# Attention with one ring of seven PSUM banks and an exponential for each score

## The chip, the core and the metric

The kernel runs on one core of a Trainium2 chip. A core has five engines that run their own instruction streams and meet through semaphores: TensorE (PE in the profile, its weight loads PEld), VectorE (DVE), ScalarE (ACT), GpSimd (POOL) and SyncE (SP), which here issues most of the transfers. Matrix products land in PSUM, here used as eight banks of 128 x 512 fp32; VectorE and ScalarE read them from there. The metric is the time of one execution on the device in microseconds; less is better.

## What is computed

A transformer block on x of shape 1 x 2048 x 448: attention with 16 query heads of 28 that share one key and one value head, and beside it an MLP, both on a layer norm of x, summed with x.

```python
x = A_x
xn = _layernorm(x, axis=-1)
return x + _A_ref(xn, A_wq, A_wk, A_wv, A_wo) + _B_ref(xn, B_w1, B_b1, B_w2, B_b2)
# _A_ref
q = (lambda x, *d: x.transpose(*d))((x @ wq).reshape(B, S, H, Dh), 0, 2, 1, 3)
k = x @ wk
v = x @ wv
scores = jnp.einsum("bhqd,bkd->bhqk", q, k) * (Dh ** -0.5)
p = _softmax(scores, axis=-1)
o = jnp.einsum("bhqk,bkd->bhqd", p, v)
return (lambda x, *d: x.transpose(*d))(o, 0, 2, 1, 3).reshape(B, S, H * Dh) @ wo
# _B_ref
y = _layernorm(x, axis=-1)
h = _gelu(jnp.einsum("bsd,df->bsf", y, w1) + b1)
return jnp.einsum("bsf,fd->bsd", h, w2) + b2
```

## The kernel before

Everything is fp32; most products use a rounded high part and a remainder. The order of each engine's work is written out by hand: instructions go to the engines' queues in the order of the Python program.

**Stages.** First layer norms and the projections to queries, keys and values (queries are parked in DRAM, `qd`). Then the MLP, with part of the attention's preparation woven in. Last, from about 500 us on, the attention stage, which alone is changed. It works in 16 units, each 512 query rows by a group of four heads, and each unit walks the 2048 keys in blocks of 128 (`kt`), two blocks per step: 128 steps, eight per unit.

**What a step issues.**
- *Scores* (`scores`, `one_score`, `single`; tile `s` or `m`): one matmul of a block of 128 keys with 512 queries of one head, then an exponential on ScalarE into half of a tile `p` (128 x 2 x 512; 13 of these, `PAIRS`). `scores` puts two scores into one tile `s` of two banks and takes one exponential over 1024 columns (L869). `single` takes one bank `m` and one exponential over 512 columns (L847); its two halves of a `p` are filled by two successive calls, kept in `halfway`. In the last `LEAD` = 11 steps the last pair of an odd step is taken apart in this way too (L862).
- *Maxima* (`max_stream`, L507 to L513; tile `m`): softmax needs each row's maximum ahead. A matmul gives 512 scores of 128 queries, and VectorE reduces them (L509). Sixteen per head; they run many units ahead of use, and the last eleven steps have none. Letter `m`.
- *Turned scores* (`turned_scores`, L541 to L549): for the fourth head of the units in `TURNED` (1 to 15) the scores are made with the queries on the partitions; VectorE writes them to SBUF with their maximum, ScalarE takes the exponential there (`turned_exp`, L560), and they go through DRAM (`td`) back as `half`. Letter `t` is one such matmul, `x` one exponential with, every second time, four stores issued from SP. The steps behind the last tile have no `t`.
- *Turned blocks* (`turn_blocks`, L834): VectorE transposes two blocks of `half` into a `p` tile. Letter `T`, two calls in an even step. So a unit in `TURNED` has six scores per step (three heads, two blocks) and takes the fourth head from `T`; unit 0 has eight scores.
- *PV* (`pv`, L820; letter `P`, only in even steps): four blocks of 128 keys with all four heads, 16 fp32 products that the profile lists as 32 matmuls, into the bank `po`. Each even step's burst takes the four blocks of the two steps before it.
- *Side work*: `n` is one move of the normalisation of a finished unit (`norm_jobs`: a copy of `po` by ScalarE, small transfers on the POOL queue, products on GpSimd), `o` one of the output projection (`o_jobs`: 12 matmuls into one bank `m`, an addition on VectorE, L735, and a store), `e` prepares the next unit's maxima (`load_max`: one transpose into a bank `m`, a copy on ScalarE and one on VectorE).

**PSUM.** In the attention stage: three banks `m` (pool `mp`, opened at the start of the kernel and shared by maxima, turned scores, singles, output projection and transposes), two tiles `s` of two banks each (pool `sp`), one bank `po` (pool `op`). A tile of a pool is given out in rotation; the matmul that writes it waits for the reader of the tile that had the bank before.

**Order.** `ORDERS[u in TURNED][n % 2]` (L29) holds one letter per piece of work: first the orders for unit 0, then for the others, each for even and odd steps; `p` is a pair of scores and `s` a single one. Maxima are dealt out by `weight` (L882): an `m` is skipped when enough of them are done for the share of the steps passed.

Of the kernel before, what the change touches and what calls it, by code (L numbers as in the profile page):

```python
# [8 lines left out]
F32 = mybir.dt.float32  # L9
F32R = mybir.dt.float32r  # L10
AF = mybir.ActivationFunctionType
ALU = mybir.AluOpType
AX = mybir.AxisListType
PSUM = bass.MemoryType.PSUM
# [11 lines left out]
BURST = 4  # L26
PAIRS = 13
MLP_MAX = 18
ORDERS = (("nmpmpmtpnompmTxP", "nmpmmpmpmepmon"), ("nsmptponmmsTxP", "nmpmmpmepmon"))  # L29
TURNED = tuple(range(1, 16))  # L30
RAWS = 2
GELU = 0.044715, 0.7978845608028654
# [6 lines left out]
def block_kernel(ctx, tc, x, wq, wk, wv, wo, w1, b1, w2, b2, out):  # L39
# [5 lines left out]
        return t.bitcast(F32)  # L45

    keep = ctx.enter_context(tc.tile_pool(name="keep", bufs=1))
    mp = ctx.enter_context(tc.tile_pool(name="mp", bufs=3, space=PSUM))
    dram = ctx.enter_context(tc.tile_pool(name="dram", bufs=1, space=bass.MemoryType.DRAM))
    xt_p = ctx.enter_context(tc.tile_pool(name="xt", bufs=2))  # L50
    qmp = ctx.enter_context(tc.tile_pool(name="qmp", bufs=1))
# [1 line left out]
    def heads_of(u):  # L53
        return 3 if u in TURNED else 4
# [56 lines left out]
    def mtile(shape):  # L111
        return mp.tile(shape, F32, name="m")
# [576 lines left out]
                    maxed += mxs.step()  # L689
    ph1b.close()  # L690
    ph1.close()

    att = ctx.enter_context(tc.tile_pool(name="att", bufs=2))
    sp = ctx.enter_context(tc.tile_pool(name="sp", bufs=2, space=PSUM))
    op = ctx.enter_context(tc.tile_pool(name="op", bufs=1, space=PSUM))

    wor = att.tile([P, NG, D], F32, name="wor", bufs=1)
# [134 lines left out]
    def turn_blocks(u, kt):  # L832
        p = pair_of()
        dve.transpose(p.rearrange("p k (g j) -> p g k j", j=32),  # L834
                      halves[u, kt // 8][:, :, 32 * (kt % 8):32 * (kt % 8) + 64].rearrange("p g (k j) -> p g k j", j=32))
        ps[u, kt, 3], ps[u, kt + 1, 3] = p[:, 0], p[:, 1]

    def pair_of():
        return att.tile([P, 2, CW], F32, name="p", bufs=PAIRS)

    halfway = []

    def one_score(u, kt, job, p):
        k, j = job
        s = mtile([P, CW])
        pe.matmul(s, ks[:, (kt + k) * P:(kt + k + 1) * P], qss[u][:, j, :], start=True, stop=True)  # L846
        act.activation(p, s, AF.Exp, scale=SCALE)  # L847
        ps[u, kt + k, j] = p

    def single(u, kt, jobs):  # L850
        if not halfway:
            halfway.extend((jobs.pop(), pair_of()))
            one_score(u, kt, halfway[0][0], halfway[1][:, 0])
        else:
            pair, p = halfway
            halfway.clear()
            one_score(u, kt, pair[1], p[:, 1])

    def scores(u, kt, jobs, apart):
        p = pair_of()  # L860
        if apart:
            for i in range(2):  # L862
                one_score(u, kt, jobs[i], p[:, i])
            return
        s = sp.tile([P, 2, CW], F32, name="s")
        for i, (k, j) in enumerate(jobs):
            pe.matmul(s[:, i], ks[:, (kt + k) * P:(kt + k + 1) * P], qss[u][:, j, :], start=True, stop=True)  # L867
            ps[u, kt + k, j] = p[:, i]
        act.activation(p, s, AF.Exp, scale=SCALE)  # L869

    def o_wait(c, gs, tiles):
        for k in range(4):
# [6 lines left out]
    pvq = [(u, kt) for u in range(NU) for kt in range(NT)]  # L879
    total = 4 * CT * len(heads)  # L880
    left = total - maxed
    weight = [0 if n >= len(steps) - LEAD else (3, 5)[n % 2] + (u == 0) for n, (u, kt) in enumerate(steps)]  # L882
    for n, (u, kt) in enumerate(steps):
        if n == 0:
            loads = pool
        if n == len(steps) - 14:
            load_rows_of(NCH - 1, range(CT))
        if u + 1 < NU and kt in ((8, 14) if u else (0, 4)):
            load_d(u + 1, kt in (4, 14))
        if 4 <= n < 4 + NG:  # L890
            prep_wo(n - 4)
        if u + 1 < NU and kt < 8:
            load_q(u + 1, (kt // 2,))
        jobs = [((0, 0), (0, 1)), ((0, 2), (1, 2)), ((1, 0), (1, 1))]
        if u not in TURNED:
            jobs[1:2] = [((0, 2), (0, 3)), ((1, 2), (1, 3))]
        for what in ORDERS[u in TURNED][n % 2]:
            if what == "s":
                single(u, kt, jobs)
            elif what == "p":  # L900
                scores(u, kt, jobs.pop(0), n % 2 == 1 and n >= len(steps) - LEAD and len(jobs) == 0)
            elif what == "m":
                if maxed < total - left + left * sum(weight[:n + 1]) / sum(weight):
                    maxed += mxs.step()
            elif what == "t":
                tq.step()
            elif what == "x":
                turned_exp()
            elif what == "T":
                for k in range(2 if u in TURNED else 0):  # L910
                    turn_blocks(u, kt + 2 * k)
            elif what == "e":
                if kt == (6 if u + 2 < NU else 10) and u + 1 < NU:
                    load_max(u + 1)
            elif what == "n":
                side.step()
            elif what == "o":
                if n == len(steps) - 5:
                    oside.add(o_jobs(NCH - 1, range(NG - 1)))
                oside.step()  # L920
            elif what == "P":
                for _ in range(BURST if n else 0):
                    pv(*pvq.pop(0))
    while pvq:
# [28 lines left out]
```

## Time and profile before

Three timed executions took 1139.23, 1139.19 and 1136.71 us, median 1139.19. The profiled execution took 1138.7 us, of which 1136.9 us lie between the first and the last instruction (its span). Busy time of each engine in stretches of the span:

| stretch (us) | what runs | PE | DVE | ACT | POOL |
|---|---|---|---|---|---|
| 300 to 400 | MLP | 98.38 | 84.70 | 64.99 | 72.78 |
| 600 to 700 | attention | 99.57 | 87.83 | 69.86 | 40.38 |
| 800 to 900 | attention | 99.00 | 80.66 | 62.97 | 35.73 |
| 1100 to 1137 | last steps and end | 31.39 | 13.10 | 15.70 | 0.79 |

The granted TensorE clock was 0.995 of full speed over the span. How to read the rows that follow: a group has the line, the engine, the operation, output and input tiles with their shapes, the count, the busy time and the mean duration in ns of one, and after the bar the idle time of the engine just before these instructions, with what ended it. A row of a timeline has the start, the duration of the merged run, the engine, the line and how many instructions were merged; in brackets the idle time before it. A matmul's duration contains its drain, so matmuls in line start closer together than their durations say. A row by stretch has the busy time and count (x) of PE, PEld, DVE, ACT and POOL, then the granted clock, the share of the DMA engines and GB/s; for one line, PE and PEld only.

### The profile page before, as it was taken

Reading aid. Unit: us, or ns where it says so; the run is one execution under the profiler, and the core shown is the slowest. Engines: PE = TensorE matmul, PEld = TensorE weight load, DVE = VectorE, ACT = ScalarE, POOL = GpSimd, SP = SyncE. Lnnn points to the kernel's source line nnn. Section 1 sums busy time; section 2 is a strip of 40 time slices with the busy share of each in tenths; the row PEclk is TensorE's granted clock in tenths of the full one; section 3 lists DMA queues with packets and bytes.
Section 4 is the critical chain, followed back from the end, with each engine's and each line's share of the span. In section 5 each row is a group of like instructions: output and inputs, shape, how many; then the busy total and the mean of one; then the engine's idle time right before and its main releaser. Section 6 shows DMA issues by size and latency. Waiting matters only on the chain.

```text
span 1136.9 us, 17010 instructions
## 1 busy us (share of the span) xinstructions
PE 1103.0 (97%) x5777; PEld 718.4 (63%) x5777; DVE 909.4 (80%) x1704; ACT 723.6 (64%) x953; POOL 564.4 (50%) x690
## 2 busy tenths in 40 slices
PE   9999899999999999999999999999999999999998
PEld 8777787877888888864544555554546444455444
DVE  7787787978888898895888887788886888866733
ACT  6765555666666666656766666467765666664673
POOL 6357787767776777772243425324432342342130
PEclk9999999999999999999999999999999999999999
DMA  8774445767776676866577797587786877975830
GB/s 273 207 226 128 123 109 129 189 172 188 195 191 169 172 204 167 206 179 152 135 176 162 175 230 197 123 206 190 161 195 164 188 169 186 225 162 124 198 85 33
DMA packets 113667, 195.11 MB, mean 172 GB/s; under 512 B 17070, under 2 KB 96100, under 8 KB 109740
## 3 DMA queue, kind: packets, MB, share of 16 engines
q1 hardware_dynamic: 100972, 172.34, 60.7%
q0 software_dynamic: 11200, 21.10, 7.4%
q8 instruction: 46, 0.75, 0.3%
q10 hardware_dynamic: 1408, 0.57, 0.2%
q14 instruction: 41, 0.34, 0.1%
HBM read 115.22 MB, written 77.71 MB: 170 GB/s over the span
## 4 chain that ended last, share of the span: by engine, by line
PE 71%; DVE 7%; DMA 6%; POOL 6%; ACT 5%; issue 2%; SPq 1%; ACTq 0%; DVEq 0%; POOLq 0%
PE po L820 19%; PE m L508 13%; PE s L867 12%; PE ph L178 6%; DVE mx L509 4%; PE m L542 4%; PE m L846 3%; PE m L622 2%; PE m L619 2%; PE m L616 2%; DMA td<-raw 2%; DMA qm<-qd 2%; POOL hx L598 1%; POOL hz L593 1%; PE qp L178 1%
## 5 line engine op out<-in xcount | busy, mean ns | idle before, releaser
L509 DVE TENSOR_REDUCE mx<-m 128x1 f32<-128x512 f32 x784 | 510.7, 685 | 97.1 <-PE m L508 85.9
L869 ACT ACTIVATE p<-s 128x1024 f32<-128x1024 f32 x326 | 315.6, 1027 | 163.0 <-PE s L867 161.6
L508 PE MATMUL m<-ks,qm 128*128 128x512 f32 x784 | 303.2, 411 | 3.0 <-DMA qm<-qd 1.9
L820 PE MATMUL po<-p,vs 128*32 128x512 f32 x2048 | 233.0, 595 | 0.0
L867 PE MATMUL s<-xh,ks 128*128 128x512 f32 x652 | 213.0, 412 | 2.7 <-ACT p L869 0.9
L508 PEld LDWEIGHTS m<-ks,qm 128*128 128x128 f32 x784 | 147.2, 189 | 89.7 <-DVE p L834 45.3
L543 DVE TENSOR_SCALAR_CACHE_REDUCE raw<-m 128x512 f32<-128x512 f32 x240 | 160.5, 689 | 31.6 <-PE m L542 12.9
L867 PEld LDWEIGHTS s<-xh,ks 128*128 128x128 f32 x652 | 114.2, 189 | 57.5 <-ACT p L869 37.2
L820 PEld LDWEIGHTS po<-p,vs 128*32 128x32 f32 x2048 | 60.0, 109 | 133.5 <-issue 132.9
L834 DVE STREAM_TRANSPOSE p<-half 128x1024 f32<-128x1024 f32 x120 | 141.6, 1218 | 3.1 <-PE po L820 3.1
L560 ACT ACTIVATE raw<-raw,m 128x1024 f32<-128x1024 f32 x120 | 133.2, 1151 | 0.0
L542 PE MATMUL m<-ks,q 128*128 128x512 f32 x240 | 97.1, 405 | 5.8 <-DVE raw L543 4.4
L603 ACT ACTIVATE hh<-hx 128x512 fp32r<-128x512 f32 x56 | 35.4, 632 | 97.5 <-POOL hx L598 97.1
L847 ACT ACTIVATE p<-m 128x512 f32<-128x512 f32 x132 | 79.0, 607 | 27.6 <-PE m L846 27.5
L605 POOL TENSOR_TENSOR hl<-hx,hh 128x512 fp32r<-128x512 f32 x56 | 72.4, 1293 | 41.6 <-ACT hh L603 41.6
L622 PE MATMUL m<-w2h,hl 128*128 128x448 f32 x224 | 83.6, 373 | 0.1
L619 PE MATMUL m<-w2l,hh 128*128 128x448 f32 x224 | 82.3, 367 | 0.0
L616 PE MATMUL m<-w2h,hh 128*128 128x448 f32 x224 | 82.0, 366 | 0.0
L593 POOL TENSOR_TENSOR hz<-hz,hx 128x512 f32<-128x512 f32 x56 | 72.5, 1296 | 4.7
L598 POOL TENSOR_TENSOR hx<-hx,hz 128x512 f32<-128x512 f32 x56 | 72.2, 1290 | 4.7
L768 POOL DMA_DIRECT2D tr<-ld x56 | 28.1, 508 | 87.6 <-DMA ld<-rc 87.6
L426 POOL DMA_DIRECT2D qm<-qd x108 | 55.2, 519 | 29.9 <-PE m L508 25.9
(167 smaller groups left out, 1504.8 us busy)
## 6 DMA issues: line engine op xcount, KB each, us to landing
td<-raw SPq DMA_DIRECT2D x240, 256.0 KB
half<-td SPq DMA_DIRECT2D x120, 512.0 KB
xh<-qd POOLq DMA_DIRECT2D x60, 168.0 KB, 7.6
a<-in_A_x_dram SPq DMA_DIRECT2D x32, 224.0 KB
qd<-qe SPq DMA_DIRECT2D x24, 256.0 KB
qm<-qd POOLq DMA_DIRECT2D x108, 56.0 KB, 6.8
qm<-qd SPq DMA_DIRECT2D x88, 56.0 KB
ad<-a SPq DMA_DIRECT2D x16, 224.0 KB
```

Source lines behind the costliest of these rows:

```text
L508: pe.matmul(pm, qm[:, t * P:(t + 1) * P], ks[:, n * CW:(n + 1) * CW], start=True, stop=True)
L509: dve.tensor_reduce(mx[:, CT * j + t, n:n + 1], pm, axis=AX.X, op=ALU.max)
L542: pe.matmul(sc, q3[i][:, t * P:(t + 1) * P], ks[:, n * CW:(n + 1) * CW], start=True, stop=True)
L543: dve.tensor_scalar(raw[:, :, 4 * n:4 * n + 4, :].rearrange("p r b i -> p b r i"), sc.rearrange("p (b r i) -> p b r i", r=4, i=32), SCALE, ...
L560: act.activation(raw[:, rs], raw[:, rs], AF.Exp, bias=m3[:, 4:5], scale=1.0)
L616: pe.matmul(m2[k], hh[:, ts], w2h[:, ft, :], start=(ft == 0), stop=False)
L619: pe.matmul(m2[k], hh[:, ts], w2l[:, ft, :], start=False, stop=False)
L622: pe.matmul(m2[k], hl[:, ts], w2h[:, ft, :], start=False, stop=(ft == NF - 1))
L820: pe.matmul(po[32 * j:32 * j + 32, :], vs[:, kt, :], ps.pop((u, kt, j)), start=(kt == 0), stop=(kt == NT - 1))
L834: dve.transpose(p.rearrange("p k (g j) -> p g k j", j=32), halves[u, kt // 8][:, :, 32 * (kt % 8):32 * (kt % 8) + 64].rearrange("p g (k j) ...
L867: pe.matmul(s[:, i], ks[:, (kt + k) * P:(kt + k + 1) * P], qss[u][:, j, :], start=True, stop=True)
L869: act.activation(p, s, AF.Exp, scale=SCALE)
```

## The change

Pool `mp` is closed at the end of the MLP stage, and pool `sp` is gone. In their place a pool `ring` of seven single banks takes the name `mp`, so scores, maxima, turned scores, output projections and transposes all rotate through the same seven; `op` keeps the eighth. Every score gets a bank and an exponential over 512 columns of its own (`score`), two successive ones share a `p` tile. The scores of a step are issued block by block, then head by head. The orders are new: six (unit 0: eight) letters `s` per step, an `m` between most of them in the first part of the step; in even steps the two turned blocks are issued one by one, the first after the second score, and the turned score comes last, just ahead of the PV burst. The `m` slots are four in even and five in odd steps (five and five in unit 0), and the weights are 4 per step (5 in unit 0) in place of 3 and 5.

```diff
@@ -26,7 +26,7 @@
 BURST = 4
 PAIRS = 13
 MLP_MAX = 18
-ORDERS = (("nmpmpmtpnompmTxP", "nmpmmpmpmepmon"), ("nsmptponmmsTxP", "nmpmmpmepmon"))
+ORDERS = (("nsmsmsnomssmsmsxtsP", "nsmsmsemssmsomsns"), ("nmsmsoTmsnxsssTtmP", "nsmsmessmmosns"))
 TURNED = tuple(range(1, 16))
 RAWS = 2
 GELU = 0.044715, 0.7978845608028654
@@ -45,7 +45,8 @@
         return t.bitcast(F32)
 
     keep = ctx.enter_context(tc.tile_pool(name="keep", bufs=1))
-    mp = ctx.enter_context(tc.tile_pool(name="mp", bufs=3, space=PSUM))
+    mpx = ExitStack()
+    mp = mpx.enter_context(tc.tile_pool(name="mp", bufs=3, space=PSUM))
     dram = ctx.enter_context(tc.tile_pool(name="dram", bufs=1, space=bass.MemoryType.DRAM))
     xt_p = ctx.enter_context(tc.tile_pool(name="xt", bufs=2))
     qmp = ctx.enter_context(tc.tile_pool(name="qmp", bufs=1))
@@ -689,9 +690,10 @@
                     maxed += mxs.step()
     ph1b.close()
     ph1.close()
+    mpx.close()
 
     att = ctx.enter_context(tc.tile_pool(name="att", bufs=2))
-    sp = ctx.enter_context(tc.tile_pool(name="sp", bufs=2, space=PSUM))
+    mp = ctx.enter_context(tc.tile_pool(name="ring", bufs=7, space=PSUM))
     op = ctx.enter_context(tc.tile_pool(name="op", bufs=1, space=PSUM))
 
     wor = att.tile([P, NG, D], F32, name="wor", bufs=1)
@@ -840,33 +842,17 @@
 
     halfway = []
 
-    def one_score(u, kt, job, p):
-        k, j = job
-        s = mtile([P, CW])
-        pe.matmul(s, ks[:, (kt + k) * P:(kt + k + 1) * P], qss[u][:, j, :], start=True, stop=True)
+    def score(u, kt, j):
+        if not halfway:
+            p = pair_of()
+            halfway.append(p[:, 1])
+            p = p[:, 0]
+        else:
+            p = halfway.pop()
+        s = mp.tile([P, CW], F32, name="m")
+        pe.matmul(s, ks[:, kt * P:(kt + 1) * P], qss[u][:, j, :], start=True, stop=True)
         act.activation(p, s, AF.Exp, scale=SCALE)
-        ps[u, kt + k, j] = p
-
-    def single(u, kt, jobs):
-        if not halfway:
-            halfway.extend((jobs.pop(), pair_of()))
-            one_score(u, kt, halfway[0][0], halfway[1][:, 0])
-        else:
-            pair, p = halfway
-            halfway.clear()
-            one_score(u, kt, pair[1], p[:, 1])
-
-    def scores(u, kt, jobs, apart):
-        p = pair_of()
-        if apart:
-            for i in range(2):
-                one_score(u, kt, jobs[i], p[:, i])
-            return
-        s = sp.tile([P, 2, CW], F32, name="s")
-        for i, (k, j) in enumerate(jobs):
-            pe.matmul(s[:, i], ks[:, (kt + k) * P:(kt + k + 1) * P], qss[u][:, j, :], start=True, stop=True)
-            ps[u, kt + k, j] = p[:, i]
-        act.activation(p, s, AF.Exp, scale=SCALE)
+        ps[u, kt, j] = p
 
     def o_wait(c, gs, tiles):
         for k in range(4):
@@ -879,7 +865,7 @@
     pvq = [(u, kt) for u in range(NU) for kt in range(NT)]
     total = 4 * CT * len(heads)
     left = total - maxed
-    weight = [0 if n >= len(steps) - LEAD else (3, 5)[n % 2] + (u == 0) for n, (u, kt) in enumerate(steps)]
+    weight = [0 if n >= len(steps) - LEAD else 4 + (u == 0) for n, (u, kt) in enumerate(steps)]
     for n, (u, kt) in enumerate(steps):
         if n == 0:
             loads = pool
@@ -891,14 +877,11 @@
             prep_wo(n - 4)
         if u + 1 < NU and kt < 8:
             load_q(u + 1, (kt // 2,))
-        jobs = [((0, 0), (0, 1)), ((0, 2), (1, 2)), ((1, 0), (1, 1))]
-        if u not in TURNED:
-            jobs[1:2] = [((0, 2), (0, 3)), ((1, 2), (1, 3))]
+        jobs = [(u, kt + k, j) for k in range(2) for j in range(heads_of(u))]
+        turns = [kt, kt + 2] if u in TURNED else []
         for what in ORDERS[u in TURNED][n % 2]:
             if what == "s":
-                single(u, kt, jobs)
-            elif what == "p":
-                scores(u, kt, jobs.pop(0), n % 2 == 1 and n >= len(steps) - LEAD and len(jobs) == 0)
+                score(*jobs.pop(0))
             elif what == "m":
                 if maxed < total - left + left * sum(weight[:n + 1]) / sum(weight):
                     maxed += mxs.step()
@@ -907,8 +890,8 @@
             elif what == "x":
                 turned_exp()
             elif what == "T":
-                for k in range(2 if u in TURNED else 0):
-                    turn_blocks(u, kt + 2 * k)
+                if turns:
+                    turn_blocks(u, turns.pop(0))
             elif what == "e":
                 if kt == (6 if u + 2 < NU else 10) and u + 1 < NU:
                     load_max(u + 1)
@@ -919,6 +902,7 @@
                     oside.add(o_jobs(NCH - 1, range(NG - 1)))
                 oside.step()
             elif what == "P":
+                assert not jobs and not turns
                 for _ in range(BURST if n else 0):
                     pv(*pvq.pop(0))
     while pvq:
```

## Prediction

> **What bounds the kernel now.** I read the page's engine totals first, then the busy time by stretch, then the groups of the attention stage, and last a timeline of one double step.
>
> ```profile
> PE 1103.0 (97%) x5777; PEld 718.4 (63%) x5777; DVE 909.4 (80%) x1704; ACT 723.6 (64%) x953; POOL 564.4 (50%) x690
> ...
> PE 71%; DVE 7%; DMA 6%; POOL 6%; ACT 5%; issue 2%; SPq 1%; ACTq 0%; DVEq 0%; POOLq 0%
> ```
>
> The totals and the chain of waits say TensorE. But its 97% contains the drain of every matmul, so small stalls hide in it. They show in the weight loads of the attention stage, the only stage that the change touches:
>
> ```profile
> L869 ACT ACTIVATE p<-s 128x1024 f32<-128x1024 f32 x314 | 304.4, 1027 | 157.7 <-PE s L867 156.3 <-PE m L508 0.2
> L509 DVE TENSOR_REDUCE mx<-m 128x1 f32<-128x512 f32 x446 | 288.6, 684 | 78.8 <-PE m L508 77.1
> ...
> L834 DVE STREAM_TRANSPOSE p<-half 128x1024 f32<-128x1024 f32 x120 | 141.6, 1218 | 3.1 <-PE po L820 3.1
> L867 PEld LDWEIGHTS s<-xh,ks 128*128 128x128 f32 x628 | 110.6, 189 | 53.2 <-ACT p L869 34.1 <-issue 3.4 <-ACT p L847 1.7
> L508 PEld LDWEIGHTS m<-ks,qm 128*128 128x128 f32 x446 | 83.2, 189 | 76.8 <-DVE p L834 45.3 <-DVE mx L509 7.7 <-issue 4.8
> L847 ACT ACTIVATE p<-m 128x512 f32<-128x512 f32 x132 | 79.0, 607 | 27.6 <-PE m L846 27.5
> ```
>
> Score loads wait 34.1 us for exponentials. (The 45.3 us put down to L834 are 54 times the same 0.84 us that follows every PV burst, also where the row says "issue": they are the burst's last matmuls, no stall.) The work repeats in double steps, an even and an odd one, with one PV burst each. One of them, with the waits that I count on:
>
> ```profile
> 742.42 3.64 PE L820 MATMUL po<-p,vs 128*32 128x512 f32 x32
> ...
> 745.99 0.19 PEld L508 LDWEIGHTS m<-ks,qm 128*128 128x128 f32 x1 [0.84 <-DVE p L834]
> 745.99 0.50 PE L508 MATMUL m<-ks,qm 128*128 128x512 f32 x1
> 746.33 0.62 PE L867 MATMUL s<-xh,ks 128*128 128x512 f32 x2
> 746.53 3.89 DVE L509 TENSOR_REDUCE mx<-m 128x1 f32<-128x512 f32 x6 [1.03 <-PE m L508]
> ...
> 747.71 0.39 PE L508 MATMUL m<-ks,qm 128*128 128x512 f32 x1
> ...
> 748.12 0.30 PEld L867 LDWEIGHTS s<-xh,ks 128*128 128x128 f32 x2 [0.45 <-ACT p L869]
> 748.13 0.73 PE L867 MATMUL s<-xh,ks 128*128 128x512 f32 x2
> ...
> 750.41 0.69 DVE L543 TENSOR_SCALAR_CACHE_REDUCE raw<-m 128x512 f32<-128x512 f32 x1
> ...
> 751.02 0.08 DVE L543 DVE_READ_ACCUMULATOR raw<-m 128x1 f32 x1
> ...
> 751.16 0.19 PEld L846 LDWEIGHTS m<-xh,ks 128*128 128x128 f32 x1 [0.30 <-DVE raw L543]
> 751.16 0.50 PE L846 MATMUL m<-xh,ks 128*128 128x512 f32 x1
> 751.60 3.64 PE L820 MATMUL po<-p,vs 128*32 128x512 f32 x32
> ```
>
> ```profile
> 742.35:751.53 9.18, 9.15 (x54) 4.57 (x53) 8.12 (x13) 7.20 (x10) 2.07 (x4) 1.00 0.99 243
> ...
> 724.20:733.20 9.00, 2.56 (x7) 1.31 (x7) 1.00 0.88 202
> ...
> 742.35:751.50 9.15, 3.02 (x8) 1.50 (x8) 1.00 0.99 242
> ```
>
> The first row is this double step as a whole (PE, PEld, DVE, ACT, POOL busy), the others count its maxima: 8 here, 7 in the earlier one. So per 9.18 us: the burst holds TensorE for 745.99 - 742.42 = 3.57, and 21 matmuls (12 scores, 8 maxima, 1 turned score) take 751.60 - 745.99 = 5.61. Unstalled they go at (747.71 - 746.33)/6 = 0.23 each. From the resumed load, the second starts at 0.34, the 21st at 0.34 + 19 x 0.23 = 4.71, and the next burst 0.33 later (0.44 after a load that stood exposed, of which 0.11 is the exposure: 0.73 against 0.62 for two). The floor is 5.04; **0.57 us of each double step is stall**, and VectorE (8.12) and ScalarE (7.20) are both below the floor of 3.57 + 5.04 = 8.61. TensorE waits for buffers, while ScalarE waits for TensorE.
>
> **The exponentials.** Two scores in one instruction become two instructions. The cost is the rate back to back, and the tail of the kernel has both forms side by side:
>
> ```profile
> 1089.28 3.64 PE L820 MATMUL po<-p,vs 128*32 128x512 f32 x32
> ...
> 1093.68 1.94 ACT L869 ACTIVATE p<-s 128x1024 f32<-128x1024 f32 x2
> ...
> 1095.50 1.59 ACT L847 ACTIVATE p<-m 128x512 f32<-128x512 f32 x3
> ...
> 1096.59 3.64 PE L820 MATMUL po<-p,vs 128*32 128x512 f32 x32
> ```
>
> A pair follows a pair after 1.94 - 1.03 = 0.91 us; a single follows a single after (1.59 - 0.607)/2 = 0.49. So a split costs 2 x 0.49 - 0.91 = 0.07 us, not 2 x 0.607 - 1.027 = 0.19. Ten singles for five pairs in a double step add 0.35 us to 7.20: ScalarE stays below the floor. The bounds of this cost are 0.46 (half a pair) and 0.607 (no overlap); I take 0.49, measured on the same instruction, though only in short runs (this one has three). The Trainium skill ("ScalarE: Activation LUTs", What ACT_TABLE_LOAD costs) gives 186 ns + 0.833 ns per element with 93 ns of overlap back to back, which is 0.52 for a single; the trace's overlap is 0.12. That becomes a rival below.
>
> **The ring.** Seven banks replace three plus two pairs; a tile now waits for the reader of the tile seven before it, whichever engine that is. I walk the new double step from its resumed load, with 8 maxima (m), 12 scores (s) and one t, in the new order. Odd step: m5 s7 m6 s8 m7 s9 s10 m8 s11 s12; even step: m1 s1 m2 s2 T m3 s3 s4 s5 s6 T t m4; burst. The first maximum starts at 746.53 - 745.99 = 0.54 (the 0.50 of its matmul and 0.04 for the signal) and each takes 3.89/6 = 0.65; an exponential starts 0.39 + 0.04 after its matmul, takes 0.60 alone and 0.49 in line; a freed bank lets the load start 0.06 later (751.16 after 751.02 + 0.08) and the matmul 0.11 after that.
> - TensorE at full pace has all ten odd tiles out by 2.18; the last three reuse banks freed by 1.20, 1.37 and 1.85.
> - VectorE ends m5, m6, m7, m8, m1, m2 at 1.20, 1.85, 2.50, 3.15, 3.80, 4.45. ScalarE ends s7 at 0.77 + 0.60 = 1.37, then s8 to s12, s1, s2 at 1.86, 2.35, 2.84, 3.33, 3.82, 4.31, 4.80.
> - The even tiles need these: m1 after s8, s1 after m7, m2 after s9, s2 after s10, m3 after m8 (3.35), s3 after s11, s4 after s12 (3.99), s5 after m1 (4.22), s6 after s1 (4.48), t after m2 (4.71), m4 after s2 (load 4.86).
> - The burst starts at 4.86 + 0.44 = **5.30**, against 5.61 now.
>
> Meanwhile VectorE does T (1.22), m3, T, t (0.69 + 0.08) and m4 from 4.45 to 8.96; the burst ends at 8.87 and the next m5 can be read at 9.41, so the transposes lie under the burst as before, with 0.45 us to spare. They now stand ahead of m3, t and m4 in VectorE's queue: a T that waited for its data would hold the ring, but its group above waited for data never (3.1 us in all, for PV). ScalarE ends s3 to s6 by 4.80 + 4 x 0.49 = 6.76, which leaves 2.1 us of the burst to the turned exponential. What is late next is ScalarE's eight exponentials in line, from s7 to s2, ahead of m4.
>
> With m4 left out (about every fourth double step has seven maxima) the burst starts at 5.04 against 9.00 - 3.57 = 5.43 now; with m8 left out instead it stays at 5.30. These lie between the following bursts, with two double steps that carry output projections from one stretch to the next:
>
> ```profile
> 547.75 3.64 PE L820 MATMUL po<-p,vs 128*32 128x512 f32 x32
> ...
> 695.22 3.64 PE L820 MATMUL po<-p,vs 128*32 128x512 f32 x32
> ...
> 724.29 3.64 PE L820 MATMUL po<-p,vs 128*32 128x512 f32 x32
> ...
> 852.91 3.64 PE L820 MATMUL po<-p,vs 128*32 128x512 f32 x32
> ...
> 881.95 3.64 PE L820 MATMUL po<-p,vs 128*32 128x512 f32 x32
> ...
> 1009.69 3.64 PE L820 MATMUL po<-p,vs 128*32 128x512 f32 x32
> ...
> 1038.09 3.64 PE L820 MATMUL po<-p,vs 128*32 128x512 f32 x32
> ...
> 1064.84 3.64 PE L820 MATMUL po<-p,vs 128*32 128x512 f32 x32
> ```
>
> Those are 16 + 14 + 14 + 3 = 47 plain ones, 9.16 us on average. The last three have no t: 26.75/3 - 3.57 = 5.35 now, 5.04 by the walk. Over the kinds (0.31, 0.39, 0.13, 0.31) I take 0.28 us. 47 x 0.28 = **13.2 us**, between 47 x 0.57 = 26.8 (the floor) and a loss (0.607 per exponential, below).
>
> **Output projection.** The six double steps with it average (29.07 + 29.04 + 28.40)/6 = 14.42.
>
> ```profile
> 701.74 0.36 PE L731 MATMUL m<-woh,oth 128*128 128x448 f32 x1
> ...
> 704.16 0.39 PE L846 MATMUL m<-xh,ks 128*128 128x512 f32 x1
> ...
> 709.16 0.19 PEld L846 LDWEIGHTS m<-xh,ks 128*128 128x128 f32 x1 [0.68 <-DVE a L735]
> ```
>
> Twelve such matmuls take 704.16 - 701.74 = 2.42, so the floor is 8.61 + 4.84 = 13.45, and 13.6 with the maxima's transpose in one of two. During those 2.42 us the readers empty the ring; the tile that waited 0.68 for VectorE's addition (one of three m banks) now has seven. I take 0.8 x 6 = **4.9 us** (0 to 5.8).
>
> **At no cost or little.** The wait for a p pair: the thirteen pairs turn over as before, and a burst frees eight at once; the transposes take their pair earlier in the step, one that the preceding burst freed. Transfers are the same, and SP and POOL get them in the same order; the turned exponential still has its four stores behind it, issued from SP. In the eleven steps without maxima, the walk gives 3.57 + 3.71 = 7.28 against 1096.59 - 1089.28 = 7.31 now, where ScalarE's 12 x 0.49 also lies under the floor; the additions there may give **1 us**. The first eight steps hold 16 scores and ten maxima a double step; 16 x 0.49 = 7.8 of ScalarE and 10 x 0.65 + 0.77 = 7.3 of VectorE lie under a floor of 3.57 + 5.04 + 6 x 0.23 = 10.0, so I put nothing there. The stage's only wait of maxima for a transfer is in these steps (us, times); with their maxima dealt out otherwise it may move by 2 us either way:
>
> ```profile
>   DMA qm<-qd: 1.9, 1
> ```
>
> The profiled run is 1138.7 us, 0.5 below the median. Sum: 1138.7 - 13.2 - 4.9 - 1 = **1119.6, so 1120 us**.
>
> **Rivals.**
> 1. *ScalarE loses the overlap* (slower). The eight exponentials in line then take 0.607 each: 0.77 + 8 x 0.607 + 0.06 + 0.44 = 6.13, so 9.70 against 9.18, and 47 x 0.52 = 24.4 lost, less 5.9 from the other terms: 1157. Against: the singles in line at 0.49. For: that run has three, and in the ring every exponential stands close behind its own matmul. The gain on plain steps is gone at (5.61 - 0.50 - 1.37)/7 = 0.534 per single; the whole kernel gets slower from about 0.55. Chance 0.25, with its milder forms.
> 2. *A single every 0.52*: the burst at 5.51, 0.10 per plain step: 1138.7 - 4.7 - 5.9 = 1128. That is the figure of the Trainium skill's section above. Chance 0.12.
> 3. *The floor*: the ring never waits: 1138.7 - 26.8 - 5.8 = 1106. For: m4 misses it by only 0.26. Against: the same chain of ScalarE. Chance 0.09.
> 4. *Transfers set the pace*: the DMA share is 0.99 in the quoted double step, and a shorter step would wait for queries or turned blocks: 1139, no change. Against: 446 maxima waited for a transfer once (1.9 us), 120 transposes never. Chance 0.06.
>
> **The numbers.** Forecast 0.48 (own range 1112 to 1127), rivals 0.25, 0.12, 0.09, 0.06. Some 0.3%, 3.4 us, is what a measurement tells from no change. Faster: 0.48 + 0.12 + 0.09 = 0.69; same 0.06; slower 0.25. The range runs from the floor and the 2 us of that transfer, 1104, up to 1148, which takes in all faster cases, no change and the lower part of the slower case.
>
> **What would show it.** Right: bursts 8.6 to 8.9 us apart in plain steps, 13.6 with output projections; single exponentials in line every 0.49; the m before a burst waiting for ScalarE; VectorE's idle time for maxima halved. Wrong: exponentials over 0.53 apart, weight loads waiting for VectorE's transposes or for DMA, bursts at 9.2 or more.

## The result and the profile after

The changed kernel takes 1146.55 us (median of six executions, 1145.22 to 1150.49), the kernel before in the same comparison 1139.21 (six, 1136.71 to 1141.84). The ratio is 1.0069 with a 95% interval of 1.0049 to 1.0089: **0.7% slower**, where 1120 was forecast. The time lies within the range on record, but the direction was wrong. The profiled execution took 1147.59 us.

The page of the changed kernel: its totals, its chain of waits by engine and by line, and one group of the stage:

```profile
PE 1101.4 (96%) x5777; PEld 721.1 (63%) x5777; DVE 892.7 (78%) x1704; ACT 740.8 (65%) x1279; POOL 564.0 (49%) x690
...
PE 56%; DMA 18%; POOL 10%; issue 7%; DVE 4%; ACT 3%; SPq 1%; POOLq 0%; DVEq 0%; ACTq 0%
PE po L822 10%; PE m L853 10%; PE m L509 9%; PE ph L179 7%; DMA ld<-rc 6%; DMA qm<-qd 4%; DMA tr<-ld 4%; PE m L543 4%; PE m L620 3%; PE m L617 3%; PE m L623 3%; POOL qm L427 2%; DMA td<-raw 2%; DMA xh<-qd 1%; POOL hx L599 1%
...
L836 DVE STREAM_TRANSPOSE p<-half 128x1024 f32<-128x1024 f32 x120 | 146.9, 1227 | 2.1 <-PE po L822 2.1
```

ScalarE's busy time grew by only 17 us and the transposes wait as little as before. But transfers hold 18% of the chain, up from 6%. Two of the lines named, `ld<-rc` (6%) and `tr<-ld` (4%), belong to one chain of side work: ScalarE copies a finished unit's sums from `po` to `oc`; its row sums are inverted in `rc` and go through DRAM (`ld`), from where `tr` spreads them over the partitions; GpSimd multiplies `oc` by `tr` and then makes the two parts `oth` and `otl` that the output projection reads.

The bursts that bounded the plain stretches of the kernel before, found again in the timeline of the changed one:

```profile
545.92 3.64 PE L822 MATMUL po<-p,vs 128*32 128x512 f32 x32
...
693.59 3.64 PE L822 MATMUL po<-p,vs 128*32 128x512 f32 x32
...
720.54 3.64 PE L822 MATMUL po<-p,vs 128*32 128x512 f32 x32
...
855.00 3.64 PE L822 MATMUL po<-p,vs 128*32 128x512 f32 x32
...
890.64 3.64 PE L822 MATMUL po<-p,vs 128*32 128x512 f32 x32
...
1016.58 3.64 PE L822 MATMUL po<-p,vs 128*32 128x512 f32 x32
...
1049.92 3.64 PE L822 MATMUL po<-p,vs 128*32 128x512 f32 x32
...
1076.49 3.64 PE L822 MATMUL po<-p,vs 128*32 128x512 f32 x32
```

The first interval (16 double steps) took 147.67 us, against 147.47: no gain. The next lost 5.8, and the output projections behind it took 35.64 against 29.04; those behind 1016.58 took 33.34 against 28.40. Three stalls do this. The first lies in the interval from 720.54 to 855.00; its timeline (start, duration, engine and line, and in brackets the idle time before and its releaser):

```profile
802.47 3.64 PE L822 MATMUL po<-p,vs 128*32 128x512 f32 x32
...
803.45 2.01 POOL L770 DMA_DIRECT2D tr<-ld  x4 [10.42 <-DMA ld<-rc]
...
803.92 1.70 SPq L706 DMA_DIRECT2D half<-td  x4
...
811.09 3.64 PE L822 MATMUL po<-p,vs 128*32 128x512 f32 x32
...
815.40 1.29 POOL L774 TENSOR_TENSOR oc<-oc,tr 128x512 f32<-128x512 f32 x1 [9.94 <-DMA tr<-ld]
...
819.42 1.26 POOL L781 TENSOR_TENSOR otl<-oc,oth 128x512 fp32r<-128x512 f32 x1
820.72 0.60 ACT L749 ACTIVATE oc<-po 128x512 f32<-128x512 f32 x1 [7.14 <-POOL otl L781]
821.85 0.29 PEld L509 LDWEIGHTS m<-ks,qm 128*128 128x128 f32 x1 [5.74 <-ACT p L854]
...
823.36 0.63 PE L509 MATMUL m<-ks,qm 128*128 128x512 f32 x1
...
824.22 0.63 PE L509 MATMUL m<-ks,qm 128*128 128x512 f32 x1
...
827.46 1.49 PE L822 MATMUL po<-p,vs 128*32 128x512 f32 x12
```

Read it upwards. ScalarE stands 7.14 us at its copy of the next unit's sums (`oc`, one buffer), because GpSimd still reads the previous unit's `oc` for `otl`. GpSimd was late because it waited 9.94 us for `tr` to land, and `tr` was issued at 803.45, just ahead of four loads of `half`, 2 MB together, at 803.92. Behind ScalarE's copy stand the exponentials, behind these the seven banks, and TensorE waits 5.74 us. The same place in the kernel before:

```profile
804.97 2.01 POOL L768 DMA_DIRECT2D tr<-ld  x4 [7.87 <-DMA ld<-rc]
806.87 3.64 PE L820 MATMUL po<-p,vs 128*32 128x512 f32 x32
...
809.00 1.28 POOL L772 TENSOR_TENSOR oc<-oc,tr 128x512 f32<-128x512 f32 x1 [2.01 <-DMA tr<-ld]
...
810.11 1.70 SPq L704 DMA_DIRECT2D half<-td  x4
...
814.20 1.30 POOL L779 TENSOR_TENSOR otl<-oc,oth 128x512 fp32r<-128x512 f32 x1
...
819.81 0.60 ACT L747 ACTIVATE oc<-po 128x512 f32<-128x512 f32 x1 [1.60 <-issue]
```

Against the burst's start, `tr` went out 1.90 us ahead (806.87 - 804.97) and now goes out 0.98 behind; the loads went out 3.24 behind and now go out 1.45 behind, since the transposes that free their buffer end earlier in the new order. So a lead of 5.14 us became 0.47. The chain had 819.81 - 815.50 = 4.3 us of margin, and the wait for `tr` grew by some 8 us.

The units of the changed kernel bear this out. In the three stalls the loads go out within 0.6 us behind `tr`, and GpSimd waits 9.6 to 10.9 us for it. In three units they go out 0.8 to 1.4 us behind, and it waits 4.9 to 6.0; in one 1.66 us behind, with 3.08; in one 3.19 us behind, with 1.88. In both kernels `tr` is also late in the three units behind output projections, where it goes out some 6 us behind a load of `half` (waits of 6.0 to 6.7 us before, 6.1 to 8.1 now). ScalarE's next copy does not wait there: in the first such unit of the kernel before, `otl` ends 7.0 us ahead of it.

The view of the copy's line in the changed kernel sums it up (idle time before it in us, times):

```profile
  POOL otl L781: 22.8, 4
```

In the kernel before this was 1.0 us, once.

### The profile page after: what moved, and what is told of

Its sections match the earlier page's. It is cut to its first block, busy times and chain, and to the rows that moved or that the text cites. A ratio compares the mean times of both kernels' runs of the same rounds, so it can differ in the third digit from the quotient of the medians.

```text
span 1145.8 us, 17203 instructions
## 1 busy us (share of the span) xinstructions
PE 1101.4 (96%) x5777; PEld 721.1 (63%) x5777; DVE 892.7 (78%) x1704; ACT 740.8 (65%) x1279; POOL 564.0 (49%) x690
## 4 chain that ended last, share of the span: by engine, by line
PE 56%; DMA 18%; POOL 10%; issue 7%; DVE 4%; ACT 3%; SPq 1%; POOLq 0%; DVEq 0%; ACTq 0%
PE po L822 10%; PE m L853 10%; PE m L509 9%; PE ph L179 7%; DMA ld<-rc 6%; DMA qm<-qd 4%; DMA tr<-ld 4%; PE m L543 4%; PE m L620 3%; PE m L617 3%; PE m L623 3%; POOL qm L427 2%; DMA td<-raw 2%; DMA xh<-qd 1%; POOL hx L599 1%
## 5 line engine op out<-in xcount | busy, mean ns | idle before, releaser
L510 DVE TENSOR_REDUCE mx<-m 128x1 f32<-128x512 f32 x784 | 505.0, 681 | 125.8 <-PE m L509 115.6
L854 ACT ACTIVATE p<-m 128x512 f32<-128x512 f32 x784 | 400.1, 626 | 166.4 <-PE m L853 164.6
L509 PE MATMUL m<-ks,qm 128*128 128x512 f32 x784 | 311.9, 407 | 20.2 <-ACT p L854 15.7
L853 PE MATMUL m<-xh,ks 128*128 128x512 f32 x784 | 277.5, 419 | 0.8 <-DVE a L627 0.8
L853 PEld LDWEIGHTS m<-xh,ks 128*128 128x128 f32 x784 | 141.0, 189 | 114.9 <-issue 42.8
L836 DVE STREAM_TRANSPOSE p<-half 128x1024 f32<-128x1024 f32 x120 | 146.9, 1227 | 2.1 <-PE po L822 2.1
L770 POOL DMA_DIRECT2D tr<-ld x56 | 28.1, 508 | 108.3 <-DMA ld<-rc 108.3
L179 PE MATMUL ph<-xh,w1h 128*128 128x512 f32 x168 | 67.0, 399 | 2.7 <-ACT hz L592 2.6
L179 PE MATMUL ph<-xh,w1l 128*128 128x512 f32 x168 | 65.7, 391 | 0.0
```

The source lines that it names most:

```text
L179: pe.matmul(ps, w, v, start=(n == 0), stop=False)
L509: pe.matmul(pm, qm[:, t * P:(t + 1) * P], ks[:, n * CW:(n + 1) * CW], start=True, stop=True)
L510: dve.tensor_reduce(mx[:, CT * j + t, n:n + 1], pm, axis=AX.X, op=ALU.max)
L836: dve.transpose(p.rearrange("p k (g j) -> p g k j", j=32), halves[u, kt // 8][:, :, 32 * (kt % 8):32 * (kt % 8) + 64].rearrange("p g (k j) ...
L853: pe.matmul(s, ks[:, kt * P:(kt + 1) * P], qss[u][:, j, :], start=True, stop=True)
```

## The experiments

Ratios are to the kernel before, run on the same chip beside each.

**1 and 2. A second `oc` buffer, in either kernel.**

```diff
-        oc = att.tile([P, CW], F32, name="oc", bufs=1)
+        oc = att.tile([P, CW], F32, name="oc", bufs=2)
```

> The changed kernel with two buffers for oc, the copy of a finished unit's PV sums, so that ScalarE's next copy need not wait for GpSimd's last product of the unit before. Theory A (plain double steps are faster as forecast, and the loss comes from three places where ScalarE's copy waits 6.5 to 8.3 us for a normalisation chain that is late): those waits are gone, the transfers of the chain are as slow as before (tr<-ld some 10 us in the bad units), bursts 8.6 to 9.7 us apart throughout, time 1120 to 1128. Rival B (the ring, the single exponentials or the lower granted clock cost the time by themselves): 1143 to 1149. Rival C (the late chain is met by the next thing that needs it, the queries' and maxima's loads behind it on the POOL queue or the output projection): 1130 to 1142.

> The kernel before with two buffers for oc. Theory A: its chain ends in time (one wait of 1.0 us in all), so nothing changes: 1137 to 1141. If the second buffer were worth something by itself, as it would be if oc had held the kernel before as well: 1125 to 1135.

Changed kernel: 1128.2 us, ratio 0.9928 (0.9903 to 0.9954), just above the 1120 to 1128 of theory A. Kernel before: 1139.79, ratio 1.0014 (1.0002 to 1.0027). So the change together with this one buffer is 0.7% faster, and the buffer alone gives nothing. ScalarE's waits for `otl` are down to one of 0.8 us. The bursts of the changed kernel with two buffers:

```profile
545.79 3.64 PE L822 MATMUL po<-p,vs 128*32 128x512 f32 x32
...
691.80 3.64 PE L822 MATMUL po<-p,vs 128*32 128x512 f32 x32
...
718.78 3.64 PE L822 MATMUL po<-p,vs 128*32 128x512 f32 x32
...
845.85 3.64 PE L822 MATMUL po<-p,vs 128*32 128x512 f32 x32
...
873.25 3.64 PE L822 MATMUL po<-p,vs 128*32 128x512 f32 x32
...
1003.06 3.64 PE L822 MATMUL po<-p,vs 128*32 128x512 f32 x32
...
1029.79 3.64 PE L822 MATMUL po<-p,vs 128*32 128x512 f32 x32
...
1056.38 3.64 PE L822 MATMUL po<-p,vs 128*32 128x512 f32 x32
```

These rows give the ledger of the prediction's terms, one profiled execution of each against that of the kernel before (us):

| term | forecast | changed kernel | with two `oc` |
|---|---|---|---|
| up to the first of these bursts | 0 | -1.8 | -2.0 |
| 47 plain double steps | -13.2 | +4.1 | -1.1 |
| 6 with output projections | -4.9 | +9.4 | -5.4 |
| behind the last | -1 | -2.8 | -2.8 |
| sum | -19.1 | +8.9 | -11.3 |

So the lack of one buffer costs 8.9 + 11.3 = 20.2 us in these executions (by the ratios 1.0069 and 0.9928 some 16 us), and even without its stalls the plain steps give almost nothing: 9.14 us on average against 9.16. Two of them, one behind the other, were stalled (11.35 and 10.44 us where their neighbours took 8.7, together 4.4): VectorE waits 2.75 us for `rc<-oc` in the first, and the burst behind it takes 5.19 us in place of 3.64, at a granted clock of 0.69. The rest is still 8 us short of the forecast.

**3. The load of the second half, one step later in the program** (still on SP).

```diff
-        if u + 1 < NU and kt in ((8, 14) if u else (0, 4)):
-            load_d(u + 1, kt in (4, 14))
+        if u + 1 < NU and kt in ((8,) if u else (0, 4)):
+            load_d(u + 1, kt == 4)
+        if u > 1 and kt == 0:
+            load_d(u, True)
```

> The changed kernel, with the load of the second half of a unit's turned blocks issued one step later in the program (at the unit's first step in place of the last step of the unit before), so that it stands behind the broadcast tr<-ld in time. Theory A1 (the chain is late because the transposes now end earlier, free their buffer earlier, and this load of 4 x 512 KB starts before the broadcast has landed): the wait for tr<-ld falls from about 10 us to 2 to 4, ScalarE's copies wait no more, time 1120 to 1128. Rival A2 (the transfers are slow because there is more traffic per time, wherever this load stands): tr<-ld stays near 10 us, time 1140 to 1149.

1146.02 us, ratio 1.0067 (1.0045 to 1.0089): nothing. The edit moved the load in the program, not in time:

```profile
802.71 2.00 POOL L770 DMA_DIRECT2D tr<-ld  x4 [10.16 <-DMA ld<-rc]
803.46 1.72 SPq L706 DMA_DIRECT2D half<-td  x4
```

So the load does not wait for its place in SyncE's program; it still starts when the transposes free its buffer. The trial says nothing on the theory.

**4. Both transposes just ahead of the burst**, so that the buffer comes free later.

```diff
-... ("nmsmsoTmsnxsssTtmP", "nsmsmessmmosns"))
+... ("nmsmsomsnxssstmTTP", "nsmsmessmmosns"))
```

> The changed kernel with both turned blocks at the end of the even step, just ahead of the burst, as in the kernel before; ring, single exponentials and the rest of the order as changed. Theory A1: the load of turned blocks starts some 2 us later, tr<-ld is ahead of it again, waits 2 to 5 us, no long wait of ScalarE's copy, time 1120 to 1130. Rival A2: as the changed kernel, 1140 to 1149.

1139.0 us (1130.45 to 1146.4), ratio 1.0012 (0.9987 to 1.0036): some 6 us better than the changed kernel by the ratios, but short of the 1120 to 1130 expected. Where the load fell behind `tr`, the wait is short; where it did not, the stall is there again:

```profile
806.25 1.29 POOL L774 TENSOR_TENSOR oc<-oc,tr 128x512 f32<-128x512 f32 x1 [1.79 <-DMA tr<-ld]
...
1009.08 0.60 ACT L749 ACTIVATE oc<-po 128x512 f32<-128x512 f32 x1 [7.03 <-POOL otl L781]
```

**5. The converse: the transposes early in the kernel before.**

```diff
-... ("nsmptponmmsTxP", "nmpmmpmepmon"))
+... ("nsmptTponmmsxP", "nmpmmpmepmon"))
```

> The kernel before with both turned blocks moved ahead in the even step, to the place right behind the turned score; banks and pairs as before. It frees the buffer of the turned blocks earlier without any ring. Theory A1: the load of turned blocks now starts ahead of the broadcast or with it, tr<-ld waits some 8 to 10 us in place of 2 in the units without output projection, and ScalarE's copies wait for GpSimd; the maxima behind the transposes wait as well (three banks): 1148 to 1165. If the transposes' place does not matter to the transfers: tr<-ld waits stay near 2 us, and only the maxima's own wait is added: 1140 to 1150.

A miss: 1137.12 us, ratio 0.998 (0.997 to 0.9991). The loads of `half` went out only 1.3 us earlier against the burst, and `tr` still led them by 2 us or more in all units but the last. So in that kernel the place of the transposes alone does not make the collision; in the changed one `tr` goes out later as well. Why `ld<-rc`, ahead of `tr`, also takes longer (a wait of 10.42 us against 7.87 in the quoted unit) was not separated.

**6. The second half loaded from ScalarE's queue, behind `tr`,** with one `oc` buffer: as in experiment 3, but issued in ScalarE's order.

```diff
+        if u > 1 and kt == 0:
+            load_d(u, True, nc.scalar)
```

> The changed kernel, one oc buffer, with the second half of a unit's turned blocks loaded from ScalarE's queue at the unit's first step, so that the load cannot start before ScalarE gets there, some 8 us after the broadcast tr<-ld was issued. (The earlier attempt left the load on SP's queue, which runs ahead of the steps, and so did not move it in time.) Theory A1: tr<-ld lands in 2 to 4 us in place of 10, ScalarE's copies wait no more than 1 us, time 1123 to 1131. Rival A2 (general traffic): tr<-ld waits stay at 8 to 11 us, 1138 to 1148.

1128.2 us, ratio 0.991 (0.9891 to 0.993). In seven of the ten units in which GpSimd waits for `tr`, it waits 1.8 to 2.1 us; the other three are those behind output projections, with 6.3 to 7.4, as in the kernel before. One copy waits for `otl`, 0.8 us:

```profile
805.44 1.29 POOL L774 TENSOR_TENSOR oc<-oc,tr 128x512 f32<-128x512 f32 x1 [1.80 <-DMA tr<-ld]
...
1039.31 5.70 ACTq L706 DMA_DIRECT2D half<-td  x3
```

The second row is the price: ScalarE issues these loads itself, mostly in some 1.7 us for four, once in over 5.7. Taking away either the collision (here, 18 us by the ratios) or the wait behind it (experiment 1, 16 us) recovers about the same: that is the cause of the direction.

**7. The ring in strict rotation** (with two `oc`). The prediction, like the part on PSUM ahead of it, took a pool's banks to be given out in rotation, so that a tile waits for the reader of the seventh tile back. The pool hands them out otherwise: counted in the program, only 536 of the stage's 1300 tiles come seven after the bank's last one, 425 come after six or fewer. Here seven pools of one bank each are taken in turn:

```diff
-    mp = ctx.enter_context(tc.tile_pool(name="ring", bufs=7, space=PSUM))
+    ring = ctx.enter_context(tc.tile_pool(name="ring", bufs=1, space=PSUM))
+
+    class Ring:
+        given = 0
+
+        def tile(self, shape, dt, name):
+            self.given += 1
+            return ring.tile(shape, dt, name=f"m{self.given % 7}")
+
+    mp = Ring()
```

> The changed kernel with two buffers for oc, and the seven banks handed out in strict rotation (seven pools of one bank, taken in turn). In the changed kernel the builder hands out the bank that it reckons free first: of 1300 tiles of the stage 536 reuse the bank of the tile seven before, 425 that of one only four to six before, 339 that of one eight to eleven before. Theory D (this uneven reuse makes TensorE wait for ScalarE and costs most of what the plain double steps fell short of the forecast): the slow double steps of 9.5 to 9.7 us fall to about 9.2 or less, plain ones average 8.9 in place of 9.08, time 1118 to 1123 against 1128 with two oc buffers alone. Rival E (the order of reuse does not matter, ScalarE's rate or the order of the letters sets the step): 1126 to 1130.

1127.72 us, ratio 0.9913 (0.9887 to 0.994). One double step of the changed kernel, the weight load of the sixth tile behind a burst and the twelve exponentials in line:

```profile
760.32 6.40 ACT L854 ACTIVATE p<-m 128x512 f32<-128x512 f32 x12 [2.90 <-PE m L853]
...
760.97 0.19 PEld L853 LDWEIGHTS m<-xh,ks 128*128 128x128 f32 x1 [0.19 <-ACT p L854]
```

and the exponentials of the same double step in strict rotation:

```profile
759.98 5.99 ACT L863 ACTIVATE p<-m 128x512 f32<-128x512 f32 x12 [3.04 <-PE m L862]
```

The sixth tile already waits for ScalarE: its load starts 0.05 us after the end of the first exponential (760.32 + 0.60), whose bank lies five tiles back. ScalarE waits for TensorE in turn: (6.40 - 0.60)/11 = 0.527 per exponential, in rotation (5.99 - 0.60)/11 = 0.49. The 9.73 us step became 8.74, as theory D has it. But the time lies in the range of rival E; it hardly fell against experiment 1, since eight double steps of 10 to 21 us, some 30 us in all over their neighbours, took the gain back. The view of waits shows maxima waiting for queries (us in all, times, longest), which is a part of it:

```profile
PE m L509 <- DMA qm<-qd: 12.0, 5, 4.3
```

**8. Rotation, and the odd step as the prediction walked it.** The walk began the odd step with a maximum; the order in the diff begins it with a score, and has four `m` there, not five as the part on the change says. Here the odd step is `nmsmsmessmmosns` (the weights deal out four of its five `m`), so the banks and the order are those of the walk:

> As the run before it in this list (two oc buffers, strict rotation), and the odd step begins with a maximum ahead of its first score: the order that the prediction walked, where the change begins the odd step with the score. The walk gave 8.87 us for a double step with eight maxima and a turned score, 8.61 without either the turned score or the last maximum. If walk and rows are right: plain ones average 8.8 to 8.9, time 1117 to 1122. If the first letter matters more than the walk shows (ScalarE starts 0.23 us later after the burst): 1123 to 1130.

1131.64 us, ratio 0.9932 (0.991 to 0.9954), above both expected ranges, with stalls of the same sort. Two bursts of a plain double step:

```profile
730.19 3.64 PE L831 MATMUL po<-p,vs 128*32 128x512 f32 x32
...
739.05 3.64 PE L831 MATMUL po<-p,vs 128*32 128x512 f32 x32
```

8.86 us apart; the walk gave 8.87 for these eight maxima, twelve scores and one turned score. So the walk's prices were right, for a ring that the kernel did not have.

**9. Single exponentials alone**, in the kernel before with its old banks:

```diff
-        act.activation(p, s, AF.Exp, scale=SCALE)
+        for i in range(2):
+            act.activation(p[:, i], s[:, i], AF.Exp, scale=SCALE)
```

> The kernel before, where each pair of scores gets two exponentials over 512 columns in place of one over 1024; banks, order and everything else as before. This prices the single exponentials alone. Forecast's row (0.07 us of ScalarE per split, a bank freed no earlier since the pair shares one tile): singles in line every 0.49 us, time 1138 to 1143. Rival 1 of the prediction (the overlap is lost, 0.607 each): 1150 to 1165.

1144.9 us, ratio 1.0058 (1.0039 to 1.0076), above the 1138 to 1143 expected. Splitting alone costs some 6.6 us in the old banks, where the score loads of pairs wait 45.4 us in all for their exponentials, against 37.2 unsplit. Whether it costs as much in the ring, which then has to earn it back, no run separates.

**10. Rotation, two `oc` and the second half from ScalarE's queue** (experiments 6 and 7 together; the last unit's half still from SP):

> Three edits on the changed kernel together: strict rotation of the seven banks, two buffers for oc, and the second half of the turned blocks loaded from ScalarE's queue at the unit's first step (for the last unit from SP as before, since ScalarE's queue stood 5.7 us in that issue in the earlier run). Theory: with rotation alone the plain steps fell to 8.5 to 8.75 us but maxima waited 12 us for their queries behind the late broadcast on the POOL queue; with the broadcast early again these waits go, and 47 plain double steps at 8.72 against 9.16 give 20 us: 1105 to 1113. If the waits for queries stay, because they come from ld<-rc and not from tr<-ld: 1118 to 1127.

A miss: 1127.45 us, ratio 0.9891 (0.9871 to 0.9912). The undisturbed plain steps took 8.74 and 8.51 us, but ScalarE's issue of the loads stretched one double step of each unit to 9.4 us or more, and once it stood 5.31 us in issuing three of them.

**11 and 12. Rotation and queries loaded two heads ahead**, with two `oc` buffers and with one. A third `qm` buffer is allocated in the attention stage:

```diff
-            qm = qmt[heads.index((u, j)) % 2]
+            qm = free.pop(0)
...
-                    if (t, n) == (0, 2) and 0 < h < len(heads) - 1:
-                        qms.append(load_m(*heads[h + 1]))
+                    if (t, n) == (0, 2):
+                        while free and h + len(qms) + 1 < len(heads):
+                            qms.append(load_m(*heads[h + len(qms) + 1]))
...
+                    if (t, n) == (CT - 1, 3):
+                        free.append(qm)
...
+    third = att.tile([P, CW], F32R, name="qm", bufs=1)
+    pool.memset(f(third), 0.0)
+    free.append(third)
```

> Changed kernel, two oc buffers, the seven banks handed out strictly in turn, and in the attention stage a third buffer for the queries of the maxima, so that they are loaded two heads ahead (some 18 us earlier) instead of one. Theory (the ring paces the plain steps at about 8.65 us on average, as the steps of the strict ring measured where nothing was late, and what the earlier strict-ring run lost, about 30 us in eight stalls with 10 to 21 us between bursts, came from queries that landed late): no wait of the maxima for their queries is left, at most two gaps over 10 us, 1100 to 1114 us. Rival (the transfers in flight are the limit, and the stalls move to another transfer, tr<-ld or the queries of the scores): queries of the maxima on time but stalls of the same sum under another name, 1122 to 1132 us.

> The kernel with the strict ring and the third query buffer, but with the one oc buffer of the changed kernel. Theory (the chain oc -> rc -> ld -> tr -> oth/otl has a margin of about 4 us in each unit, less in a faster kernel, and the second oc buffer is what hides a late tr<-ld): ScalarE's copy waits for otl again, 5 to 9 us in three or more units, 10 to 30 us above the kernel with two buffers. Rival (with the queries early nothing collides any longer): within 4 us of the kernel with two buffers, no copy wait over 2 us.

With two buffers 1126.37 us (1121.18 to 1131.17), ratio 0.9895 (0.9873 to 0.9918): with experiment 10 the lowest ratio measured, but short of the 1100 to 1114 expected. Queries no longer matter (one wait of 2.6 us); the stalls came back under another name, as the rival said. The largest, 18.70 us between bursts, in its profiled execution (1121.18 us):

```profile
966.26 2.79 SPq L721 DMA_DIRECT2D half<-td  x4
966.91 0.73 POOL L776 DMA_DIRECT2D rc<-oc  x1
...
976.74 0.25 DVE L779 RECIPROCAL rc<-rc 128x16 f32<-128x16 f32 x1 [9.26 <-DMA rc<-oc]
...
977.59 0.50 PEld L868 LDWEIGHTS m<-xh,ks 128*128 128x128 f32 x2 [9.53 <-DVE mx L511]
```

Again a small transfer goes out beside 2 MB of `half`, this time `rc<-oc`. VectorE waits 9.26 us at the reciprocal, the reductions of the maxima stand behind it, and the ring behind these. The long stretches without a stall show what the ring gives: 16 double steps from 545.21 to 685.63 us, 8.78 on average against 9.22 before.

With one buffer 1138.88 us, ratio 1.0004 (0.9986 to 1.0022): 12.5 us more, as its theory expected, and the stall of the changed kernel again:

```profile
813.04 1.26 POOL L789 TENSOR_TENSOR oc<-oc,tr 128x512 f32<-128x512 f32 x1 [11.39 <-DMA tr<-ld]
...
818.33 0.60 ACT L764 ACTIVATE oc<-po 128x512 f32<-128x512 f32 x1 [9.61 <-POOL otl L796]
```

So the best version tried is about 1.1% faster than the kernel before. A kernel in which no small transfer meets a load of `half`, without ScalarE paying for it, was not tried.

## Why the prediction was wrong

**Right.** ScalarE's pace: 0.49 per single in line was taken from three, and holds over twelve (experiment 7), so rivals 1 (0.607) and 2 (0.52) fall. The Trainium skill ("ScalarE: Activation LUTs", What ACT_TABLE_LOAD costs) gives 93 ns of overlap for activations back to back; over long lines too the trace's is 0.12 us (0.607 - 0.49). The walk's step of 8.87 (8.86 in experiment 8). The output projection: 4.9 forecast, 5.4 in experiment 1, where the stalls are gone. The transposes behind which the ring might stand: they waited 2.1 us in all.

**The step that gave the wrong sign** is the sentence "Transfers are the same, and SP and POOL get them in the same order". They are the same in the program, and not in time: with the transposes ending earlier in the step, the `half` buffer came free 1.8 us earlier against the burst, while `tr` went out 2.9 later. What the moved transposes wait for was priced, what their end sets free was not. The margin stood in the profile of before: in the quoted unit `otl` ended 4.3 us ahead of the copy that needs its buffer, with a wait of 2.01 us for `tr`. That cost 20.2 us between the profiled executions. The rivals missed it too: the fourth, transfers that set the pace, looked at queries and turned blocks, priced "no change", and left out the small transfers of the normalisation; the slower one was about ScalarE. That the range still held the time was luck: its upper end, 1148, stood for no change and the milder forms of a slower ScalarE, and that is not what came.

**The term that was mis-sized** is 0.28 us per plain double step. In the changed kernel without the stalls (experiment 1) it is (1.1 + 4.4)/47 = 0.12. Its premise, "a tile now waits for the reader of the tile seven before it", does not hold for this pool (experiment 7). The order was misread as well: the real odd step, which begins with a score, gives 8.74 in rotation where the walk's gives 8.86, so that this slip made the forecast gain smaller and not larger.

**Nothing was put** on the steps up to the first quoted burst, which gave 1.8, and 1 us on the end, which gave 2.8. Both helped the forecast, but the first is no more than the spread: over the variants of the changed kernel this burst starts between 543.30 (experiment 7) and 549.49 us (experiment 12), against 547.75 before.

**Still open**: which of the later `ld`, its slower landing and the earlier loads weighs most in the shift against the burst, since experiment 5 moved only the last of these. The slower landing is not enough for a stall: in experiment 6 GpSimd waits 110.2 us in all for `ld<-rc`, against 108.3 in the changed kernel and 87.6 before, and those three stalls are gone. That the order of the banks holds the plain steps to 0.12 us is shown by single double steps (9.73 against 8.74), and not by the time of a whole execution, which other stalls set in experiments 7 to 11.

## What to carry to other kernels

Before a reordering is priced, look at the side chains that share an in-order engine with the main loop, and write down the margin of each (when its buffer comes free, when it is next written): here one buffer behind a margin of 4.3 us stood between a gain of 0.7% and a loss of 0.7%. A transfer of an engine that runs ahead, as SyncE did here (experiment 3), starts when its buffer comes free, not where it stands in the program, so a step that moves a reader moves a transfer. And how many buffers a pool has does not say which one comes next: count it in the program, or take single buffers in turn.

## What the runs showed of the hardware

A small transfer beside a large one: `tr` among the transfers issued between 800 and 816 us in the changed kernel (KB each, median us to landing), beside the four loads of 512 KB:

```profile
tr<-ld POOLq DMA_DIRECT2D x4, 64.0 KB, 7.2
```

against, in experiment 6 in the same stretch, with the loads 4 us behind:

```profile
tr<-ld POOLq DMA_DIRECT2D x4, 64.0 KB, 2.1
```

The Trainium skill ("DMA: Bandwidth & Descriptors", Queues, rings and completion order) says that each DMA engine goes round between the queues that have work, a packet at a time; taken alone, that lets one expect a small transfer to slip through. The measured 7.2 us, and GpSimd's waits of up to 11.96 (experiment 4, with the loads 0.25 us behind), say that it doesn't here.

A stall costs more than its length. In the stall quoted first, the matmuls behind it start (824.22 - 823.36)/2 = 0.43 apart, with a score between the two maxima quoted, where 0.23 is the rate; this lasts some 5 us, so that a wait of 5.74 became a double step of 827.46 - 811.09 = 16.37. The granted clock of that stretch (the number behind the busy times), in the changed kernel:

```profile
800.00:900.00 100.00, 88.21 (x489) 50.34 (x492) 67.36 (x109) 56.56 (x110) 29.93 (x50) 0.93 0.68 157
```

0.93 with two such stalls, where the same 100 us of the kernel before had 1.00; from 821.00 to 827.46 alone it is 0.57. By the Trainium skill ("TensorE: Matmul & The Clock Gate", What's actually happening) the clock is halved after an idle window of some 3.4 us, until TensorE has been busy about as long. The trace agrees with the halving, with 0.43 against 0.23 after a wait of 5.74 us; the slow stretch lasted some 5 us here.

ScalarE can stand in issuing a load: four loads of 512 KB took it some 1.7 us as a rule, and 5.3 and 5.7 us for three of them in experiments 10 and 6.
